# Decode attention with a gated MLP on one core: the small matrix products computed with moving weights in column groups

## The chip, the core and the metric

The kernel runs on one core of one Trainium2 chip. The metric is the time of one execution in device microseconds. Before the change its median over three runs is 1341.24 us (1341.04 to 1341.56). The profile shows one such execution by engine: PE is TensorE (PEld its weight loads), DVE is VectorE, ACT is ScalarE, POOL is GpSimd, SP is SyncE, which here does nothing but issue DMA transfers.

## The reference

Two batch rows, each with a single new token. One branch is attention over a long cache, the other a two-stage MLP; a sigmoid gate mixes them.

```python
# B = 2, Sq = 1, D = 1024, H = 32, Sk = 16384, Dh = 128, F = 3584; all inputs bf16
g = sigmoid((x * gate_w).sum(-1))
q = (x @ wq).reshape(B, 1, H, Dh)
p = softmax(q . k_cache * Dh ** -0.5)          # per head, over 16384 positions
a = (p . v_cache).reshape(B, 1, H * Dh) @ wo
h = gelu(layernorm(x) @ w1)
hs = shift(h) @ w2      # with one position, the four shifted quarters are all padding: zeros
x1 = x + hs
b = x1 + gelu(layernorm(x1) @ w3) @ w4
out = g * a + (1 - g) * b
```

The caches make up nearly all of the bytes: 2 x 32 heads x 16384 x 128 x 2 bytes is 268 MB for K and as much for V. wq and wo have 8.4 MB each, w3 and w4 7.3 MB each, w1 and w2 2.1 MB each.

## The kernel before

**Units.** The work on the caches is cut into 32 units; a unit is a pair of heads of one batch row, and its K and its V are 8.4 MB each: 128 partitions of 64 KB. One large SBUF tile, `mem`, has five cells of 32 KB a partition. K of even units lies in cells 0 and 1, K of odd units in cells 1 and 2, V in cells 3 and 4 (the V of unit 30 in cells 0 and 1). Before the units begin, cells 3 and 4 hold wq, cell 2 holds w1 and w2; then w3 comes into cells 3 and 4 over wq, then w4 over w3, then V of unit 0 over w4. So each of these transfers waits until PE has read what it overwrites.

**The queue.** All loads are issued by SP in one order: wq, x, gate_w, w1, w2, K0, w3 (two halves), K1, the first pair of wo, w4 (two halves), K2, V0 (two halves), K3, V1, K4, V2 and so on. An issue that waits holds up all behind it. K of unit n+1 is issued when the first half of the scores of unit n has been transposed, since the two share a cell.

**A unit (loop at L630).** `score_chunks` (L454) transposes K in eight chunks on DVE (L462, 32x32 blocks of 32-bit words) and multiplies each on PE with 8 weight loads and 8 matmuls of 512 columns (L468), all into one PSUM bank `S`. `softmax_a` transposes S (L489), takes the maximum (L491) and spreads it through a diagonal matrix made by ACT (L493); `softmax_b` sums that on PE (L499), reduces it on DVE (L505) and computes the exponentials on ACT (L507); `softmax_c` sums them on PE (L521) and takes the reciprocal on DVE (L523). `pv_moving` (L539) multiplies the probabilities with V two units later: V moves, 512 columns at a time, through four column groups of the PE array (the output lies at partitions 0, 32, 64 and 96 of the PSUM bank `oacc`), with the 8 probabilities of a position group as weights. `pv_rows` (L554) masks and adds the four parts of `oacc` on DVE, and a small matmul with `hsel` (L590, L585) sums the partitions. After each second unit `wo_project` (L438) adds the heads' part of the output to `arow`, a PSUM tile in which the 1024 output columns lie as four column groups of 256.

**The q product and the MLP layers.** q (L266 to L275) and `LinearT.compute` (L228) use weights as the stationary operand: for each 128 output columns and each 128 rows a weight load of 128x128 and a matmul of only 2 columns (the two batch rows). The outputs then lie along the partitions, as later steps want them. For the MLP layers the 128 columns of one weight load are a column step of C elements apart in memory (C = 8 for w1, w2 and w4, 28 for w3). The q result is spread over partitions by four matmuls with the selection matrices `sel` (L141) into `qd`, of which POOL makes the padded weights `qw` (L301).

**Where the third and fourth layer stand.** w3 is loaded and computed in two halves of its rows. In unit 0 the first half is computed in two parts around `softmax_b` (L640, L642), the second after `softmax_c` (L645); w4's halves are loaded as w3's become free (L643, L646). Unit 1 does the same with w4, and loads the two halves of V0 as w4's become free (L652, L655). The order of the instructions of one engine is worked out by the framework's scheduler, which also moves matmuls of the layers between those of the scores.

**The end.** The V of the last unit comes in nine pieces (`PIECES`, L106: seven of 32 position blocks and two of 16), and then four pieces of wo (L432). `pv_last` (L603) uses the first three pieces as moving operand and the other six as stationary (L612), adds the masked sum of the moving part first (L609), scales (L619) and projects the last two head pairs (L620). DVE copies one half of the columns of `arow` to SBUF, ACT the other (L677, L678), and two stores follow, one per batch row (L680).

Of the kernel before, what the change touches and what calls it, by code (L numbers as in the profile page):

```python
# [10 lines left out]
FP32 = mybir.dt.float32  # L11
# [12 lines left out]
def kernel(  # L24
# [74 lines left out]
    def load_v(u):  # L99
        nc.sync.dma_start(out=region(v_cell[u], NJ * Dh), in_=cache_rows(A_v_cache, u))  # L100

    def load_v_half(u, k):
        at = slice(k * CELL, (k + 1) * CELL)
        nc.sync.dma_start(out=region(v_cell[u], NJ * Dh)[:, at], in_=cache_rows(A_v_cache, u)[:, at])

    PIECES = [32] * 7 + [16] * 2  # L106
    assert sum(PIECES) == NJ

# [29 lines left out]
    ones_f = const.tile([P, P], FP32)  # L138
    nc.vector.memset(ones_f[:], 1.0)

    sel = const.tile([P, 4, Q4, QP], BF16)  # L141
    nc.gpsimd.memset(sel[:], 0.0)
    for v in range(4):
        w, e = divmod(v, 2)
        nc.gpsimd.affine_select(
            out=sel[:, v],
            in_=sel[:, v],
            compare_op=ALU.not_equal,
            fill=1.0,
            base=-(2 * QP * w + e),  # L150
            pattern=[[0, Q4], [-2, QP]],
            channel_multiplier=1,
        )
    mask4 = const.tile([P, Q4], BF16)
    nc.gpsimd.memset(mask4[:], 1.0)
    nc.gpsimd.affine_select(
# [46 lines left out]
    for k in range(NP):  # L203
        t = const.tile([P, NJ // 4, 2, 4], BF16, name=f"pt{k}")
        nc.gpsimd.memset(t[:], 0.0)
        pts.append(t)

    class LinearT:

        def __init__(self, W, actT, name, cell, offset, nparts=1):  # L210
            self.actT = actT
            K, self.N = W.shape
            self.R = K // P
            self.C = self.N // P
            self.rows = self.R // nparts
            self.src = W.rearrange("(p r) n -> p (r n)", p=P)

            self.at = [(cell + k) * CELL + offset for k in range(nparts)]
            self.acc = mlp.tile([P, self.C, B], FP32, name=f"{name}_acc")

        def part(self, k):
            return mem[:, self.at[k] : self.at[k] + self.rows * self.N]

        def load(self, k=0):
            n = self.rows * self.N
            nc.sync.dma_start(out=self.part(k), in_=self.src[:, k * n : (k + 1) * n])

        def compute(self, k, c0, c1):  # L228
            wc = self.part(k).rearrange("p (r n) -> p r n", n=self.N)
            ps = misc_psum([P, c1 - c0, B])  # L230
            for c in range(c0, c1):
                for r in range(self.rows):
                    nc.tensor.matmul(  # L233
                        ps[:, c - c0, :],
                        lhsT=wc[:, r, :].rearrange("p (m c) -> p c m", c=self.C)[:, c, :],
                        rhs=self.actT[:, k * self.rows + r, :],
                        start=(r == 0),
                        stop=(r == self.rows - 1),
                    )
            acc = self.acc[:, c0:c1, :]  # L240
            if k == 0:
                nc.vector.tensor_copy(out=acc, in_=ps[:])
            else:
                nc.vector.tensor_tensor(out=acc, in0=acc, in1=ps[:], op=ALU.add)

    xn1T = mlp.tile([P, KC, B], BF16)
    hT = mlp.tile([P, KC, B], BF16)
# [5 lines left out]

    lin1 = LinearT(B_w1, xn1T, "w1", 2, 0)
    lin2 = LinearT(B_w2, shT, "w2", 2, KC * D)
    lin3 = LinearT(B_w3, xn2T, "w3", 3, 0, 2)
    lin4 = LinearT(B_w4, h2T, "w4", 3, 0, 2)
    lin1.load()
    lin2.load()
    load_k(0)  # L260
# [1 line left out]
    xT = const.tile([P, KC, B], BF16)  # L262
    nc.vector.tensor_copy(out=xT[:], in_=xin[:].rearrange("p b r -> p r b"))  # L263

    qps = misc_psum([P, H, B])
    for h in range(H):  # L266
        for r in range(KC):
            nc.tensor.matmul(  # L268
                qps[:, h, :],
                lhsT=wq_t[:, r, h * Dh : (h + 1) * Dh],  # L270
                rhs=xT[:, r, :],
                start=(r == 0),
                stop=(r == KC - 1),
            )
    lin3.load(0)  # L275
    lin3.load(1)
    qT = const.tile([P, H, B], BF16)
    nc.vector.tensor_copy(out=qT[:], in_=qps[:])
    qdps = misc_psum([P, 4, H * B])
    for v in range(4):  # L280
        nc.tensor.matmul(
            qdps[:, v, :],
            lhsT=sel[:, v].rearrange("p a k -> p (a k)"),
            rhs=qT[:].rearrange("p h b -> p (h b)"),
            start=True,
            stop=True,
        )

    qd = const.tile([P, HP, B, 4], BF16)
    for e in range(2):  # L290
        rows = slice(e * HALF, (e + 1) * HALF)
        nc.vector.tensor_copy(
            out=qd[rows],
            in_=qdps[rows].rearrange("p v (hp e b) -> p hp e b v", e=2, b=B)[:, :, e],
        )
    qdu = qd[:].rearrange("p hp b v -> p (hp b) v")

    def write_qw(u):
# [82 lines left out]
        layernorm_T(x1T[:], xn2T[:], "ln2")  # L381


    NQ = D // Q4
    arow_t = rps.tile([P, NQ], FP32, name="arow")
    nc.vector.memset(arow_t[:], 0.0)
    arow = [arow_t[QP * k : QP * k + B, :] for k in range(Q4)]

    def mlp_post4():

        omg = mlp.tile([P, B], FP32, name="omg")
        nc.vector.tensor_scalar(
            out=omg[:], in0=g_rep[:], scalar1=-1.0, scalar2=1.0, op0=ALU.mult, op1=ALU.add
        )
        nc.vector.tensor_tensor(out=bT[:], in0=lin4.acc[:], in1=x1T[:], op=ALU.add)
        nc.vector.tensor_tensor(
            out=bT[:], in0=bT[:], in1=omg[:].unsqueeze(1).to_broadcast([P, KC, B]), op=ALU.mult
        )
        W = NQ // KC
        for k in range(Q4):  # L400
            for c in range(KC):
                nc.tensor.matmul(  # L402
                    arow[k].rearrange("b (m c) -> b c m", c=KC)[:, c, :],
                    lhsT=bT[:, c, :],
                    rhs=ident_f[:, k * W : (k + 1) * W],
                    start=(c == 0),
                    stop=False,
                    skip_group_check=True,
                )
# [27 lines left out]

    def wo_project(hp):  # L438
        for r in range(2):
            for k in range(Q4):  # L440
                nc.tensor.matmul(
                    arow[k],
                    lhsT=OT[:, hp, r, :],
                    rhs=wo_tiles[hp, r][:, k * NQ : (k + 1) * NQ],
                    start=False,
                    stop=(hp == HP - 1 and r == 1),
                    skip_group_check=True,
                )
# [154 lines left out]
    def pv_last(u):  # L603
        hp, b = units[u]
        ot = misc_psum([P, 2])
        moving = sum(PIECES[:3]) // 4
        pv_moving(u, 0, moving, moving)
        red = pv_rows(u, mask4m)
        nc.tensor.matmul(ot[:], lhsT=red[:, 0:Dh], rhs=hsel[:], start=True, stop=False)  # L609
        V = v_view(u)  # L610
        for j in range(4 * moving, NJ):
            nc.tensor.matmul(  # L612
                ot[:],
                lhsT=V[:, j, :],
                rhs=pts[u % NP][:, j // 4, :, j % 4],
                start=False,
                stop=(j == NJ - 1),
            )
        nc.vector.tensor_tensor(out=OT[:, hp, :, b], in0=ot[:], in1=rinvs[u % NP][:], op=ALU.mult)  # L619
        for k in range(HP - LASTP, HP):  # L620
            wo_project(k)

    compute_gate()
    layernorm_T(xT[:], xn1T[:], "ln1")
    lin1.compute(0, 0, lin1.C)
    mlp_post1()
    lin2.compute(0, 0, lin2.C)
    mlp_post2()

    for n in range(NU):  # L630
# [6 lines left out]
        softmax_a(n)  # L637
        if n == 0:
            load_wo_pair(0)
            lin3.compute(0, 0, FC // 2)  # L640
            softmax_b(n)
            lin3.compute(0, FC // 2, FC)  # L642
            lin4.load(0)  # L643
            softmax_c(n)
            lin3.compute(1, 0, FC)  # L645
            lin4.load(1)  # L646
            gelu_T(lin3.acc[:], h2T[:], FC)
        elif n == 1:
            lin4.compute(0, 0, KC // 2)
            softmax_b(n)  # L650
            lin4.compute(0, KC // 2, KC)
            load_v_half(0, 0)  # L652
            softmax_c(n)
            lin4.compute(1, 0, KC)
            load_v_half(0, 1)  # L655
            mlp_post4()
        else:
            pv(n - 2)
            if n < NU - 1:
                load_v(n - 1)  # L660
            else:
                load_v_pieces(NU - 1)
            pv_end(n - 2)
            if n == NU - 1:
                load_wo_last()
            softmax_b(n)
            softmax_c(n)
# [3 lines left out]
    pv_end(NU - 2)  # L671
    pv_last(NU - 1)

    out_row = mlp.tile([P, NQ], BF16)
    used = slice(0, QP * (Q4 - 1) + B)
    half = NQ // 2
    nc.vector.tensor_copy(out=out_row[used, 0:half], in_=arow_t[used, 0:half])  # L677
    nc.scalar.activation(out=out_row[used, half:NQ], in_=arow_t[used, half:NQ], func=ACTF.Copy)  # L678
    for b, queue in ((0, nc.sync), (1, nc.scalar)):
        queue.dma_start(  # L680
            out=out[b, 0].rearrange("(k n) -> k n", k=Q4),
            in_=out_row[b : b + QP * (Q4 - 1) + 1 : QP, :],
        )


# [28 lines left out]
```

## Time and profile before

| what | value |
|---|---|
| median of three runs | 1341.24 us |
| the profiled execution | 1341.09 us, its span 1339.4 us |
| PE busy / PEld / DVE / ACT | 768.8 / 351.9 / 705.1 / 105.2 us |
| moved by DMA | 573.33 MB, mean 428 GB/s over the span |
| L268 (q), 256 matmuls | 7.1 us busy |
| L233 (layers), weight loads, 576 | 36.9 us busy |
| last V piece used by PE (L612) | 1332.80 us |
| last stores issued (L680) | 1336.49 us |

The page gives busy times of the engines, the share of the DMA engines in 40 equal slices of the span, a chain that follows the last instruction back to what released it, and groups of instructions with their mean duration. The timeline lists instructions in order of time, merged: start, time until the end of the last of them, engine, line, operation, output and inputs, count, and in brackets the idle time of the engine before them with what ended it. "Clock" is the TensorE clock that was granted, as a part of full speed.

### The profile page before, as it was taken

What the parts mean: (1) busy time and instruction counts of PE and PEld (TensorE: products, weight loads), DVE (VectorE), ACT (ScalarE), POOL (GpSimd) and SP (SyncE); (2) the same over time, 40 slices, a digit from 0 to 9 for tenths busy, and PEclk for the clock granted to TensorE, in tenths of its full rate; (3) what the DMA queues carried; (4) which work ended last, traced back from release to release, by engine and by line L of the source; (5) the groups of instructions that cost most, each with busy time, mean ns of one, the idle gap of its engine ahead of it and who ended that gap; (6) DMA issues with size and microseconds to landing.
All of it is one profiled execution on the core that took longest, in us unless ns stands there. A gap on an engine that the chain in (4) does not pass through costs nothing.

```text
span 1339.4 us, 12490 instructions
## 1 busy us (share of the span) xinstructions
PE 768.8 (57%) x5502; PEld 351.9 (26%) x5502; DVE 705.1 (53%) x695; ACT 105.2 (8%) x165; POOL 15.2 (1%) x54
## 2 busy tenths in 40 slices
PE   2688566554566645556654546665455665555564
PEld 2456222222222212222222212222122222222222
DVE  1445566554556554556655445656444665545561
ACT  0011000000000000000000000000000000000000
POOL 1000000000000000000000000000000000000000
PEclk9977887776788777788877778877678886777886
DMA  9999999999999999999999999999999999999997
GB/s 406 425 429 432 440 431 433 435 423 440 429 435 437 429 429 437 425 435 435 435 431 429 429 437 431 429 427 430 440 431 431 427 433 423 437 435 435 433 423 309
DMA packets 14486, 573.33 MB, mean 428 GB/s; under 512 B 1880, under 2 KB 1888, under 8 KB 4448
## 3 DMA queue, kind: packets, MB, share of 16 engines
q1 hardware_dynamic: 14424, 572.54, 99.3%
q8 instruction: 43, 0.70, 0.2%
q14 instruction: 11, 0.09, 0.0%
q10 hardware_dynamic: 8, 0.00, 0.0%
HBM read 572.53 MB, written 0.00 MB: 427 GB/s over the span
## 4 chain that ended last, share of the span: by engine, by line
DMA 67%; PE 16%; DVE 12%; issue 4%; ACT 0%; another core or an unknown queue 0%; POOL 0%; SPq 0%; ACTq 0%; DVEq 0%
DMA mem<-in_A_k_cache_dram 62%; PE S L468 12%; DVE KT L462 12%; PE misc L233 2%; DMA mem<-in_A_v_cache_dram 2%; DMA xin<-in_A_x_dram 2%; DMA wo<-in_A_wo_dram 1%; PE misc L268 1%; ACT pt L507 0%; PE arow L402 0%; PE oacc L543 0%; DVE St L489 0%; POOL ln_rstd L350 0%; PE misc L344 0%
## 5 line engine op out<-in xcount | busy, mean ns | idle before, releaser
L468 PE MATMUL S<-KT,qw 128*128 128x512 bf16 x2048 | 544.2, 415 | 369.5 <-DVE KT L462 369.3
L462 DVE STREAM_TRANSPOSE KT<-mem 128x2048 f32<-128x2048 f32 x256 | 570.9, 2283 | 271.7 <-DMA mem<-in_A_k_cache_dram 219.5
L468 PEld LDWEIGHTS <-qw 128*128 128x128 bf16 x2048 | 217.7, 107 | 688.3 <-issue 509.2
L543 PE MATMUL oacc<-mem,pt 128*8 128x512 bf16 x2008 | 116.9, 384 | 8.7 <-DMA mem<-in_A_v_cache_dram 8.7
L507 ACT ACTIVATE pt<-St,nb 64x256 bf16<-64x256 f32 x64 | 90.0, 1406 | 149.5 <-DVE nb L505 148.6
L493 ACT ACTIVATE Dm<-ident_s,m 128x128 f32<-128x128 f32 x32 | 12.8, 401 | 998.8 <-DVE m L491 998.8
L521 PE MATMUL misc<-rs,lmat 128*128 128x1 f32 x62 | 18.2, 362 | 85.8 <-ACT pt L507 85.6
L543 PEld LDWEIGHTS <-pt 128*8 128x8 bf16 x2008 | 46.4, 87 | 76.2 <-issue 25.9
L489 DVE STREAM_TRANSPOSE St<-S 128x512 f32<-128x512 f32 x32 | 22.9, 717 | 66.6 <-PE S L468 66.6
L523 DVE RECIPROCAL rinv<-misc 128x1 f32<-128x1 f32 x31 | 5.2, 169 | 96.3 <-PE misc L521 96.3
L559 DVE TENSOR_SCALAR part<-oacc,maskr 128x128 f32<-128x128 f32 x31 | 10.9, 351 | 83.0 <-PE oacc L543 83.0
L590 PE MATMUL misc<-hsel,red 128*128 128x2 f32 x112 | 17.5, 261 | 51.5 <-DVE red L565 51.5
L521 PEld LDWEIGHTS misc<-rs,lmat 128*128 128x128 f32 x62 | 15.5, 310 | 94.2 <-ACT pt L507 94.2
L233 PEld LDWEIGHTS <-mem 128*128 128x128 bf16 x576 | 36.9, 169 | 2.2 <-issue 1.4
L590 PEld LDWEIGHTS misc<-hsel,red 128*128 128x128 f32 x112 | 15.9, 202 | 64.8 <-issue 62.6
L507 ACT ACTIVATION_READ_ACCUMULATOR pt<-St,nb 64x1 f32 x64 | 30.7, 480 | 0.0
L565 DVE SCALAR_TENSOR_TENSOR part<-oacc,maskr,part 128x128 f32<-128x128 f32 x62 | 21.8, 351 | 2.2
L268 PE MATMUL misc<-xT,mem 128*128 128x2 bf16 x256 | 7.1, 165 | 26.1 <-DVE xT L263 23.5
L301 POOL TENSOR_TENSOR qw<-qd,mask 128x16 bf16<-128x16 bf16 x32 | 8.4, 264 | 1188.1 <-PE S L468 1159.5
L599 DVE CAST OT<-misc 64x2 bf16<-64x2 f32 x56 | 9.0, 160 | 22.9 <-PE misc L590 22.6
L499 PE MATMUL misc<-Dm,ones_f 128*128 128x128 f32 x64 | 16.5, 343 | 3.5 <-ACT Dm L493 3.5
L505 DVE TENSOR_REDUCE nb<-misc 64x1 f32<-64x64 f32 x64 | 14.2, 222 | 5.5 <-PE misc L499 3.5
(97 smaller groups left out, 150.7 us busy)
## 6 DMA issues: line engine op xcount, KB each, us to landing
mem<-in_B_w_dram SPq DMA_DIRECT2D x4, 3584.0 KB, 18.8
mem<-in_A_v_cache_dram SPq DMA_DIRECT2D x2, 4096.0 KB
wo<-in_A_wo_dram SPq DMA_DIRECT2D x7, 1024.0 KB, 32.4
mem<-in_A_v_cache_dram SPq DMA_DIRECT2D x7, 1024.0 KB, 24.7
mem<-in_B_w_dram SPq DMA_DIRECT2D x2, 2048.0 KB, 28.6
mem<-in_A_v_cache_dram SPq DMA_DIRECT2D x2, 512.0 KB, 17.9
wo<-in_A_wo_dram SPq DMA_DIRECT2D x4, 256.0 KB, 12.8
mem<-in_A_k_cache_dram SPq DMA_DIRECT2D x32, 28.2
```

What stands on the lines that cost most here:

```text
L233: nc.tensor.matmul(ps[:, c - c0, :], lhsT=wc[:, r, :].rearrange("p (m c) -> p c m", c=self.C)[:, c, :], rhs=self.actT[:, k * self.rows + r ...
L268: nc.tensor.matmul(qps[:, h, :], lhsT=wq_t[:, r, h * Dh : (h + 1) * Dh], rhs=xT[:, r, :], start=(r == 0), stop=(r == KC - 1),)
L462: nc.vector.transpose(out=kt[:], in_=Kc.rearrange("p j d -> p (j d)").bitcast(FP32))
L468: nc.tensor.matmul(S, lhsT=t[:, v, NG - 1 - m : NG - 1 - m + P], rhs=ktb[:, half * GT : (half + 1) * GT, w, :, e], start=(first and n == 0 ...
L489: nc.vector.transpose(out=st[:].rearrange("p j r -> p (j r)"), in_=S[:])
L499: nc.tensor.matmul(R_ps[:], lhsT=ones_f[:], rhs=Dm[:], start=True, stop=True)
L505: nc.vector.tensor_reduce(out=nb[rows], in_=R_ps[rows, rows], axis=AX.X, op=ALU.min)
L507: nc.scalar.activation(out=Pt[rows, :, e, :].rearrange("p (m a) k -> p a k m", a=GT // 4), in_=st[rows, :, 0:NG].rearrange("p (a k) m -> p ...
L521: nc.tensor.matmul(tot_ps[:, 0:1], lhsT=lmat[:], rhs=rs[:], start=True, stop=True)
L543: nc.tensor.matmul(acc[QP * q : QP * q + 8, :], lhsT=pts[u % NP][:, g].rearrange("p h k -> p (h k)"), rhs=v_view(u)[:, 4 * g : 4 * g + 4, ...
L565: nc.vector.scalar_tensor_tensor(out=red[:] if twice else part[:], in0=in0.unsqueeze(1).to_broadcast([P, 2, Dh]) if twice else in0, scalar ...
L590: nc.tensor.matmul(ot[:, r, :], lhsT=red[:, r : 2 * Dh : 2], rhs=hsel[:], start=True, stop=True,)
```

## The change

The q product and the four layers swap the roles of their operands. The 2 columns of the activations become the stationary operand, and the weights move, up to 512 columns in a matmul, in four column groups, accumulating in the two banks of `oacc`. The result lies in rows 0 and 1 of each group of 32 partitions; DVE transposes the whole bank in 32x32 blocks (`flipped`) and copies the wanted columns. With that the outputs lie along the partitions as before. `sel` and its matmuls are gone. For q the moving columns are runs of 128 contiguous ones, and column groups 0 and 1 compute the same heads, as do 2 and 3; for the layers the columns of a matmul step by C elements.

w3 and w4 are loaded and computed whole: the third layer after the scores of unit 0, w4's load behind it; the fourth layer in unit 1, and V0's load, whole, behind it. In the program after scheduling the third layer's matmuls stand behind all scores of unit 0 and ahead of its softmax sum; the fourth layer's stand behind the sum of exponentials (L508 in the changed kernel) of unit 1.

In the last unit all pieces of V but the last two move, and the masked sum is added after the stationary part. In the program after scheduling, both pairs of the last projection stand behind that. `arow` becomes two tiles, each of two rows and 512 columns, in column groups 0 and 1 of two PSUM banks; each of DVE and ACT copies and stores one of them.

```diff
-    sel = const.tile([P, 4, Q4, QP], BF16)
-    nc.gpsimd.memset(sel[:], 0.0)
-    for v in range(4):
...
+    def flip():
+        flips[0] += 1
+        return oacc[flips[0] % 2]
+
+    def flipped(acc, view):
+        t = mlp.tile([P, 512], FP32, tag="flip", name="flip")
+        src = view(acc)
+        n = src.shape[1] * src.shape[2] * (src.shape[3] if len(src.shape) > 3 else 1)
+        nc.vector.transpose(out=t[:, 0:n], in_=src)
+        return t[:, 0:n].rearrange("p (c k) -> p c k", k=QP)[:, :, 0:B]
...
-        def compute(self, k, c0, c1):
-            wc = self.part(k).rearrange("p (r n) -> p r n", n=self.N)
-            ps = misc_psum([P, c1 - c0, B])
-            for c in range(c0, c1):
-                for r in range(self.rows):
-                    nc.tensor.matmul(
-                        ps[:, c - c0, :],
-                        lhsT=wc[:, r, :].rearrange("p (m c) -> p c m", c=self.C)[:, c, :],
-                        rhs=self.actT[:, k * self.rows + r, :],
...
+        def compute(self):
+            wc = self.dst.rearrange("p (r g k c) -> p r g c k", g=Q4, k=QP, c=self.C)
+            step = min(self.C, 512 // QP)
+            while self.C % step:
+                step -= 1
+            for c0 in range(0, self.C, step):
+                acc = flip()
+                for r in range(self.R):
+                    for g in range(Q4):
+                        nc.tensor.matmul(
+                            acc[QP * g : QP * g + B, 0 : step * QP],
+                            lhsT=self.actT[:, r, :],
+                            rhs=wc[:, r, g, c0 : c0 + step, :],
+                            start=(r == 0),
+                            stop=(r == self.R - 1),
+                        )
+                got = flipped(
+                    acc, lambda a: a[:, 0 : step * QP].rearrange("p (c k) -> p c k", k=QP)
+                )
+                nc.vector.tensor_copy(out=self.acc[:, c0 : c0 + step, :], in_=got)
...
+    qd = const.tile([P, HP, B, 4], BF16)
+    HG = 512 // Dh
+    for h0 in range(0, HP, HG):
+        acc = flip()
         for r in range(KC):
+            for g in range(Q4):
+                nc.tensor.matmul(
+                    acc[QP * g : QP * g + B, :],
+                    lhsT=xT[:, r, :],
+                    rhs=wq_t[:, r, :].rearrange("p (hp e d) -> p hp e d", e=2, d=Dh)[
+                        :, h0 : h0 + HG, g // 2, :
+                    ],
+                    start=(r == 0),
+                    stop=(r == KC - 1),
+                )
+        got = flipped(acc, lambda a: a[:].rearrange("p (c k e) -> p c e k", k=QP, e=2))
         nc.vector.tensor_copy(
+            out=qd[:, h0 : h0 + HG],
+            in_=got.rearrange("p (hp v) b -> p hp b v", v=4),
+        )
+    lin3.load()
...
-    NQ = D // Q4
-    arow_t = rps.tile([P, NQ], FP32, name="arow")
-    nc.vector.memset(arow_t[:], 0.0)
-    arow = [arow_t[QP * k : QP * k + B, :] for k in range(Q4)]
+    NH2 = D // 512
+    arow_t = [rps.tile([QP * k + B, 512], FP32, name=f"arow{k}") for k in range(NH2)]
+    arow = [arow_t[k][QP * k : QP * k + B, :] for k in range(NH2)]
...
-            for k in range(Q4):
+            for k in range(NH2):
                 nc.tensor.matmul(
                     arow[k],
                     lhsT=OT[:, hp, r, :],
-                    rhs=wo_tiles[hp, r][:, k * NQ : (k + 1) * NQ],
+                    rhs=wo_tiles[hp, r][:, k * 512 : (k + 1) * 512],
...
     def pv_last(u):
-        moving = sum(PIECES[:3]) // 4
+        moving = sum(PIECES[:-2]) // 4
         pv_moving(u, 0, moving, moving)
         red = pv_rows(u, mask4m)
-        nc.tensor.matmul(ot[:], lhsT=red[:, 0:Dh], rhs=hsel[:], start=True, stop=False)
...
+        for k in range(HP - LASTP, HP - 1):
+            wo_project(k)
+        nc.tensor.matmul(ot[:], lhsT=red[:, 0:Dh], rhs=hsel[:], start=False, stop=True)
         nc.vector.tensor_tensor(out=OT[:, hp, :, b], in0=ot[:], in1=rinvs[u % NP][:], op=ALU.mult)
-        for k in range(HP - LASTP, HP):
-            wo_project(k)
+        wo_project(HP - 1)
...
         if n == 0:
             load_wo_pair(0)
-            lin3.compute(0, 0, FC // 2)
+            lin3.compute()
+            lin4.load()
             softmax_b(n)
-            lin3.compute(0, FC // 2, FC)
-            lin4.load(0)
+            gelu_T(lin3.acc[:], h2T[:], FC)
             softmax_c(n)
-            lin3.compute(1, 0, FC)
-            lin4.load(1)
-            gelu_T(lin3.acc[:], h2T[:], FC)
         elif n == 1:
-            lin4.compute(0, 0, KC // 2)
+            lin4.compute()
+            load_v(0)
             softmax_b(n)
-            lin4.compute(0, KC // 2, KC)
-            load_v_half(0, 0)
+            mlp_post4()
             softmax_c(n)
-            lin4.compute(1, 0, KC)
-            load_v_half(0, 1)
-            mlp_post4()
...
-    nc.vector.tensor_copy(out=out_row[used, 0:half], in_=arow_t[used, 0:half])
-    nc.scalar.activation(out=out_row[used, half:NQ], in_=arow_t[used, half:NQ], func=ACTF.Copy)
...
+    nc.vector.tensor_copy(out=out_row[0:B, :], in_=arow[0])
+    nc.sync.dma_start(out=rows[:, 0:512], in_=out_row[0:B, :])
+    nc.scalar.activation(out=out_row[QP : QP + B, :], in_=arow[1], func=ACTF.Copy)
+    nc.scalar.dma_start(out=rows[:, 512:1024], in_=out_row[QP : QP + B, :])
```

More of the change, by code (lines that the diff above doesn't have):

```diff
@@ L100, in load_v @@
         nc.sync.dma_start(out=region(v_cell[u], NJ * Dh), in_=cache_rows(A_v_cache, u))
-    def load_v_half(u, k):
-        at = slice(k * CELL, (k + 1) * CELL)
-        nc.sync.dma_start(out=region(v_cell[u], NJ * Dh)[:, at], in_=cache_rows(A_v_cache, u)[:, at])
     PIECES = [32] * 7 + [16] * 2
@@ L139 @@
     nc.vector.memset(ones_f[:], 1.0)
-    sel = const.tile([P, 4, Q4, QP], BF16)
-    nc.gpsimd.memset(sel[:], 0.0)
-    for v in range(4):
[L144 to L153, printed above, removed]
     mask4 = const.tile([P, Q4], BF16)
@@ L206, with __init__ @@
         pts.append(t)
+    flips = [0]
+    def flip():
[7 more added lines that the diff above has]
+        return t[:, 0:n].rearrange("p (c k) -> p c k", k=QP)[:, :, 0:B]
     class LinearT:
-        def __init__(self, W, actT, name, cell, offset, nparts=1):
+        def __init__(self, W, actT, name, cell, offset):
             self.actT = actT
@@ L214, in __init__ @@
             self.C = self.N // P
-            self.rows = self.R // nparts
             self.src = W.rearrange("(p r) n -> p (r n)", p=P)
-            self.at = [(cell + k) * CELL + offset for k in range(nparts)]
+            at = cell * CELL + offset
+            self.dst = mem[:, at : at + self.R * self.N]
             self.acc = mlp.tile([P, self.C, B], FP32, name=f"{name}_acc")
[L221 to L226, printed above, removed]
@@ L228, in compute, with load @@
-        def compute(self, k, c0, c1):
-            wc = self.part(k).rearrange("p (r n) -> p r n", n=self.N)
-            ps = misc_psum([P, c1 - c0, B])
-            for c in range(c0, c1):
-                for r in range(self.rows):
-                    nc.tensor.matmul(
-                        ps[:, c - c0, :],
-                        lhsT=wc[:, r, :].rearrange("p (m c) -> p c m", c=self.C)[:, c, :],
-                        rhs=self.actT[:, k * self.rows + r, :],
[L237 to L244, printed above, removed]
+        def load(self):
+            nc.sync.dma_start(out=self.dst, in_=self.src)
@@ L255 @@
     lin2 = LinearT(B_w2, shT, "w2", 2, KC * D)
-    lin3 = LinearT(B_w3, xn2T, "w3", 3, 0, 2)
-    lin4 = LinearT(B_w4, h2T, "w4", 3, 0, 2)
+    lin3 = LinearT(B_w3, xn2T, "w3", 3, 0)
+    lin4 = LinearT(B_w4, h2T, "w4", 3, 0)
     lin1.load()
@@ L263 @@
     nc.vector.tensor_copy(out=xT[:], in_=xin[:].rearrange("p b r -> p r b"))
-    qps = misc_psum([P, H, B])
-    for h in range(H):
+    qd = const.tile([P, HP, B, 4], BF16)
+    HG = 512 // Dh
+    for h0 in range(0, HP, HG):
+        acc = flip()
         for r in range(KC):
[L268 to L286, printed above, removed]
-        )
[L289 to L295, printed above, removed]
+            for g in range(Q4):
[9 more added lines that the diff above has]
+        got = flipped(acc, lambda a: a[:].rearrange("p (c k e) -> p c e k", k=QP, e=2))
+        nc.vector.tensor_copy(
+            out=qd[:, h0 : h0 + HG],
+            in_=got.rearrange("p (hp v) b -> p hp b v", v=4),
+        )
+    lin3.load()
     qdu = qd[:].rearrange("p hp b v -> p (hp b) v")
@@ L398, in mlp_post4 @@
         )
-        W = NQ // KC
-        for k in range(Q4):
+        W = 512 // KC
+        for k in range(NH2):
             for c in range(KC):
@@ L439, in wo_project @@
         for r in range(2):
-            for k in range(Q4):
+            for k in range(NH2):
                 nc.tensor.matmul(
@@ L615, in pv_last @@
                 rhs=pts[u % NP][:, j // 4, :, j % 4],
-                start=False,
-                stop=(j == NJ - 1),
-            )
+                start=(j == 4 * moving),
+                stop=False,
+            )
+        for k in range(HP - LASTP, HP - 1):
+            wo_project(k)
+        nc.tensor.matmul(ot[:], lhsT=red[:, 0:Dh], rhs=hsel[:], start=False, stop=True)
         nc.vector.tensor_tensor(out=OT[:, hp, :, b], in0=ot[:], in1=rinvs[u % NP][:], op=ALU.mult)
-        for k in range(HP - LASTP, HP):
-            wo_project(k)
+        wo_project(HP - 1)
     compute_gate()
     layernorm_T(xT[:], xn1T[:], "ln1")
-    lin1.compute(0, 0, lin1.C)
+    lin1.compute()
     mlp_post1()
-    lin2.compute(0, 0, lin2.C)
+    lin2.compute()
     mlp_post2()
@@ L672 @@
     pv_last(NU - 1)
[L674 to L683, printed above, removed]
+    out_row = mlp.tile([QP + B, 512], BF16)
+    rows = out.rearrange("b s d -> (b s) d")
+    nc.vector.tensor_copy(out=out_row[0:B, :], in_=arow[0])
+    nc.sync.dma_start(out=rows[:, 0:512], in_=out_row[0:B, :])
+    nc.scalar.activation(out=out_row[QP : QP + B, :], in_=arow[1], func=ACTF.Copy)
+    nc.scalar.dma_start(out=rows[:, 512:1024], in_=out_row[QP : QP + B, :])
 _INS = ['A_x', 'A_k_cache', 'A_v_cache', 'A_wq', 'A_wo', 'B_x', 'B_w1', 'B_w2', 'B_w3', 'B_w4', 'gate_w']
```

## The prediction

> **What bounds the kernel now.** I read the page's slices, then the chain of waits, then windows over the trace.
>
> ```profile
> DMA  9999999999999999999999999999999999999997
> ...
> DMA 67%; PE 16%; DVE 12%; issue 4%; ACT 0%; another core or an unknown queue 0%; POOL 0%; SPq 0%; ACTq 0%; DVEq 0%
> ```
> ```profile
> 52.00:92.00 40.00, 32.00 (x292) 21.69 (x292) 21.28 (x20) 3.46 (x6) 0.26 (x1) 0.87 1.00 428
> 92.00:132.00 40.00, 33.53 (x355) 23.49 (x355) 23.66 (x23) 3.52 (x6) 0.26 (x1) 0.76 1.01 433
> 172.00:1324.00 1152.00, 657.61 (x4169) 275.71 (x4167) 630.20 (x587) 93.03 (x145) 7.13 (x27) 0.78 1.00 431
> ```
> The last two columns of a window are the busy share of the DMA engines and GB/s. They stand at 1.00 and about 430 in the stage of the MLP as in the steady loop. In the packet records of the trace all 16 engines have a packet in flight from 1.9 us until the tail, and a 64 KB packet takes 2.42 us (16 x 65,536 B / 2.42 us = 433 GB/s). So the time is bytes over that rate, plus the head, plus the tail. PE or DVE time saved in between buys nothing; PE time added costs only when it makes SP issue a transfer after the queue has run dry. So I read SP's issues in the timeline next:
>
> ```profile
> 64.42 0.33 SPq L97 DMA_DIRECT2D mem<-in_A_k_cache_dram  x1
> ...
> 83.35 7.85 SPq L226 DMA_DIRECT2D mem<-in_B_w_dram  x2
> 102.99 0.33 SPq L97 DMA_DIRECT2D mem<-in_A_k_cache_dram  x1
> 121.31 7.77 SPq L104 DMA_DIRECT2D mem<-in_A_v_cache_dram  x2
> ```
> In the packet records these transfers (K1, w4, K2, V0) move their first packets at 68.17, 90.37, 107.12 and 126.09, when the work queued ahead is drained. The very first transfer needed 1.0 us from issue (0.79) to packet (1.81). So the latest harmless issues are 67.1, 89.3, 106.1 and 125.1; w3, issued at 33.1, has until 49.5.
>
> **Head: q, first and second layer.** Removed: 256 q matmuls (23.48 to 33.2), four `sel` matmuls and three casts; 2 x 64 matmuls of the layers at 62 ns (7.97 us). Added: 128 q matmuls of 512 columns, 2 x 32 of 256, and six flips. Four column groups at once are in the trace at V:
>
> ```profile
> 1255.96 3.63 PE L543 MATMUL oacc<-mem,pt 128*8 128x512 bf16 x64
> ...
> 1312.92 6.60 PE L543 MATMUL oacc<-mem,pt 128*8 128x512 bf16 x80 [8.65 <-DMA mem<-in_A_v_cache_dram]
> ...
> 1313.30 0.14 PEld L543 LDWEIGHTS <-pt 128*8 128x8 bf16 x4 [0.28 <-issue]
> ```
> Warm, a round of four takes 3.63/16 = 0.227 us; after an idle PE 0.14+0.28 = 0.42, for some ten rounds. q: 32 rounds, 10 x 0.42 + 22 x 0.227 = 9.2 us, so it ends near 32.7 and w3 goes out where it does now, 16 us early. A flip is like L489's transpose of 128x512 from PSUM, 0.72 us; the four hide under the next rounds but for the last. A layer of 8 rounds of 256 columns takes 8 x 0.21 = 1.7 cold plus about 0.6 for flip and copy, against 4.15; xn2T is ready near 45 instead of 49.9. All of it hides behind K0, whose last packet ends at 52.97: 0. At the price of the old strided weight loads (4 us a layer, the bound above) xn2T is ready near 51: still 0. POOL loses `sel`, DVE the clearing of arow; neither queue is waited for before 23 us: 0.
>
> **Third layer and w4.** In place of 224 matmuls, part of them woven between the scores of unit 0, 64 of 448 columns run after those scores. Without them unit 0 should go like a late unit: first K transpose 1234.24, last score 1256.0, 21.8 us; 53.45 + 21.8 = 75.3. Its 16 rounds at 448/512 x 0.227 = 0.20 take 3.2 us, so w4, now one transfer instead of two, goes out at 78.5 (limit 89.3). The weights step 56 bytes between columns, and no moving operand of the trace does; the nearest in step are L233's weight loads:
>
> ```profile
> 23.48 6.09 PE L268 MATMUL misc<-xT,mem 128*128 128x2 bf16 x223 [23.48 <-DVE xT L263]
> ...
> 38.00 7.77 PEld L233 LDWEIGHTS <-mem 128*128 128x128 bf16 x128 [1.40 <-issue]
> ```
> 61 ns for 128 stepped columns against 27 for contiguous ones. At 0.48 ns a column for all four groups together the layer costs 64 x 448 x 0.48 = 13.8 us, w4 goes out at 89.1: just in time. So 0 at both ends here.
>
> **Fourth layer and V0: the thin place.** V0 overwrites the weights, so it waits for the whole layer. PE's order in the changed program puts the 112 matmuls behind the normalising sum (L521), which waits for ACT's exponentials; the halves of the old layer stood around it:
>
> ```profile
> 121.41 0.50 PEld L521 LDWEIGHTS misc<-rs,lmat 128*128 128x128 f32 x2 [0.22 <-ACT pt L507]
> ...
> 121.65 6.99 PEld L233 LDWEIGHTS <-mem 128*128 128x128 bf16 x112
> ```
> K1's last packet ends at 89.5; transposes from 90.0, scores until 111.8 (21.8 as above). Last score to the sum's end took 115.7 to 122.0, so 6.3: the layer starts at 118.1 on a cold PE. 28 rounds of 256 columns at 0.21 = 6.0 us, so V0 goes out at 124.1, 1.0 us before the limit: 0. Ends of the range: 28 x 0.113 = 3.2 us warm (0 as well); or 112 x 256 x 0.48 = 13.8 us by L233. In that case the third layer's 13.8 us also push the softmax of unit 0, whose reciprocal stands ahead of K1's transposes on DVE: they begin near 94.2, scores end at 116.0, the layer runs from 122.3 to 136.1, and DMA stands still for 11.0 us. I take the cold L543 row, alike in form and state. Behind V0 on SP stands K3, due 14 us later in the old run; K2's transposes on DVE wait for the layer's flip and bT, done near 126, and K2 lands at 128.5.
>
> [...]
>
> **Bytes and packets.** Order rows for PE fall from 10,494 to 9,239. Instruction fetch (0.79 MB for 12,490 instructions, 64 B each) shrinks by 80 KB, five 16 KB packets of 1.07 us: 5 x 1.07/16 = -0.33 us. w3, w4 and V0 move in packets twice as large: 512 packets of 28 KB at 1.064 us become 256 at about 2.12 (-0.13), 256 of 32 KB at 1.215 become 128 at 2.42 (-0.08).
>
> **Tail.**
>
> ```profile
> 1332.80 0.59 PE L612 MATMUL misc<-pt,mem 128*128 128x2 bf16 x16 [0.68 <-DMA mem<-in_A_v_cache_dram]
> ...
> 1333.42 0.16 DVE L619 TENSOR_TENSOR OT<-misc,rinv 128x2 bf16<-128x2 f32 x1 [10.34 <-PE misc L612]
> ...
> 1335.42 0.38 PE L441 MATMUL arow<-wo,OT 128*2 128x256 bf16 x4 [0.26 <-DMA wo<-in_A_wo_dram]
> ...
> 1335.86 0.29 DVE L677 CAST out_row<-arow 98x128 bf16<-98x128 f32 x1 [2.27 <-PE arow L441]
> 1336.18 0.28 ACT L678 ACTIVATE out_row<-arow 98x128 bf16<-98x128 f32 x1 [32.82 <-DVE out_row L677]
> 1336.49 1.35 ACTq L680 DMA_DIRECT2D out_dram<-out_row  x1
> ```
> The last wo piece decides, not V. Four V pieces turn from 32 stationary matmuls (1.01 us) into 8 moving ones (two rounds, 0.6 to 1.0), 2.45 us apart: hidden. The masked sum now follows the seventh piece: 1330.3 + 1.0 + 1.65 (as 1321.45 to 1323.09) = 1333.0; its product with hsel runs behind the last V matmul, 1333.4 to 1333.8, and OT is written at 1334.06 instead of 1333.58. The last two pieces of wo land at 1334.78 and 1335.42: 0.7 us of cover, beyond which lateness would count in full. Two groups of 512 columns take 0.43 cold where four of 256 took 0.21: +0.21 on the last one (0 if warm). Copies: DVE by L278's 64 columns (0.22) and L677's 128 (0.29) is 1.1 ns a column, so 512 take 0.71; ACT from L678 by 0.5 to 0.8 ns a column 0.47 to 0.6. Now ACT waits for DVE and both stores wait for ACT, 0.63 us after the matmuls; then each engine copies and stores its own half, ACT, whose store ends last, after 0.6, DVE after 0.7. Together +0.2 (0 to +0.5).
>
> **Sum.** Span 1339.4 - 0.33 - 0.21 + 0.2 = 1339.06. The profiled run took 1341.09 around its span (+1.69), and the median stands 0.15 higher: 1340.9.
>
> **Rivals.** *Forecast, no change to speak of* (0.74): 1340.3 to 1341.8. *V0 late* (0.18): slower from the point where the fourth layer takes over 7.0 us, 62 ns a matmul where I have 53. If column groups with stepped weights ran two at a time, 56 x 0.21 = 11.8 us, the gap is 4.9 and the time 1345.8; at L233's rate 1352. For it: the thin place, and the 61 ns row; against: four streams together at V. *A tail that gets longer* (0.05): OT behind the last wo piece by up to 0.5, copies one after the other as now, +0.6: about 1342; L677 to L678 speaks for it, two separate PSUM tiles against. *A real gain* (0.03): the woven layers were in somebody's way after all; the full DMA share from 12 to 1324 us leaves only head and tail, some 6 us, so 1338 at best.
>
> This kernel can't tell less than about 0.2%, 2.7 us, from no change. Of V0-late I put 0.04 below that: same 0.74 + 0.04 + 0.05 = 0.83, slower 0.14, faster 0.03. Range 1340.2 to 1346.0: it takes in two-at-a-time and leaves out L233's price (about 0.06) and the gain.
>
> **What would show it.** V0's issue before 125 and DMA at 1.00 in 92 to 172 us: right; a slice below and V0 after 126: the rival. Also w4's issue near 79, the old landing of K0 and K1, the last wo matmul to the stores in about 0.8 us more or less unchanged. A DMA gap anywhere else, or packets slower than 2.42 us, would make the whole reasoning wrong.

## The result and the profile after

The changed kernel takes 1346.62 us (median of six runs, 1346.15 to 1347.11) against 1341.16 (six runs of the kernel before): 5.5 us more, a ratio of 1.004 with a 95% interval of 1.0027 to 1.0053. The profiled execution took 1346.30 us, its span 1344.5 against 1339.4.

Windows of the trace after, over the stage of the MLP and over the steady loop (the last three columns are granted clock, DMA share and GB/s):

```profile
52.00:92.00 40.00, 30.53 (x132) 8.95 (x132) 22.09 (x23) 3.46 (x6) 0.27 (x1) 0.88 0.99 423
92.00:132.00 40.00, 30.81 (x180) 10.96 (x179) 19.83 (x15) 3.21 (x5) 0.26 (x1) 0.83 0.86 370
...
172.00:1324.00 1152.00, 663.24 (x4052) 274.26 (x4055) 630.22 (x579) 93.07 (x145) 7.17 (x27) 0.77 1.00 432
```

One window alone lost DMA time: 0.86 where the kernel before had 1.01. Narrower windows show an outright stop, with PE busy all through it:

```profile
126.00:128.00 2.00, 2.00 (x24) 0.67 (x20) 0.00 (x0) 0.00 (x0) 0.00 (x0) 1.00 0.04 8
128.00:130.00 2.00, 2.00 (x21) 0.54 (x16) 0.00 (x0) 0.00 (x0) 0.00 (x0) 1.00 0.00 0
130.00:132.00 2.00, 2.00 (x20) 0.41 (x12) 0.00 (x0) 0.00 (x0) 0.00 (x0) 1.00 0.00 0
```

The timeline after, for the third layer with w4's issue and for the fourth with V0's:

```profile
74.89 12.39 PE L231 MATMUL oacc<-mem,xn2T 128*2 128x448 bf16 x64
...
87.32 0.33 SPq L219 DMA_DIRECT2D mem<-in_B_w_dram  x1
...
119.22 12.88 PE L231 MATMUL oacc<-mem,h2T 128*2 128x256 bf16 x112
...
132.14 0.33 SPq L100 DMA_DIRECT2D mem<-in_A_v_cache_dram  x1
```

The fourth layer takes 12.9 us, not 6. V0, which overwrites its weights, goes out at its end, 132.1, when more than half of the DMA engines have had no packet for 5.5 us (the last one ran dry at 128.1); its first packets follow a microsecond later. By the packet records fewer than half of the DMA engines are at work from 126.66 to 133.24, 6.6 us. Everything later is DMA-bound again, so none of it comes back. The rest of the difference goes the other way. The last load ends at 1340.22 instead of 1334.95; without the 6.6 us that would be 1333.6, 1.3 earlier. And from that point to the end of the span it is 4.28 us instead of 4.45. 6.6 - 1.3 - 0.2 = 5.1, the difference of the spans.

### The profile page after: what moved, and what is told of

Same layout as the page of the kernel before. It is cut to its first block, busy times and chain, and to the rows that moved or that the text cites. A ratio compares the mean times of both kernels' runs of the same rounds, so it can differ in the third digit from the quotient of the medians.

```text
span 1344.5 us, 11160 instructions
## 1 busy us (share of the span) xinstructions
PE 776.2 (58%) x4842; PEld 315.2 (23%) x4842; DVE 710.1 (53%) x701; ACT 105.2 (8%) x165; POOL 13.8 (1%) x49
## 4 chain that ended last, share of the span: by engine, by line
DMA 67%; PE 15%; DVE 13%; issue 4%; another core or an unknown queue 0%; ACT 0%; POOL 0%; SPq 0%; DVEq 0%; ACTq 0%
DMA mem<-in_A_k_cache_dram 62%; DVE KT L449 12%; PE S L455 11%; DMA mem<-in_A_v_cache_dram 3%; PE oacc L231 2%; DMA xin<-in_A_x_dram 2%; PE oacc L269 1%; ACT pt L494 0%; DVE flip L203 0%; PE arow L428 0%; POOL ln_rstd L338 0%; PE misc L508 0%; PE misc L332 0%; DVE St L476 0%
## 5 line engine op out<-in xcount | busy, mean ns | idle before, releaser
L530 PE MATMUL oacc<-mem,pt 128*8 128x512 bf16 x2040 | 122.0, 392 | 16.1 <-DMA mem<-in_A_v_cache_dram 16.1
L480 ACT ACTIVATE Dm<-ident_s,m 128x128 f32<-128x128 f32 x32 | 12.9, 402 | 1000.7 <-DVE m L478 1000.7
L508 PE MATMUL misc<-rs,lmat 128*128 128x1 f32 x62 | 18.0, 359 | 86.8 <-ACT pt L494 86.8
L508 PEld LDWEIGHTS misc<-rs,lmat 128*128 128x128 f32 x62 | 15.4, 308 | 101.2 <-ACT pt L494 101.2
L203 DVE STREAM_TRANSPOSE flip<-oacc 128x512 f32<-128x512 f32 (+2 forms) x9 | 5.5, 613 | 34.0 <-PE oacc L231 28.4
L269 PE MATMUL oacc<-mem,xT 128*2 128x512 bf16 x128 | 8.8, 445 | 23.2 <-DVE xT L260 23.2
```

Source lines behind the costliest of these rows:

```text
L269: nc.tensor.matmul(acc[QP * g : QP * g + B, :], lhsT=xT[:, r, :], rhs=wq_t[:, r, :].rearrange("p (hp e d) -> p hp e d", e=2, d=Dh)[:, h0 : ...
L508: nc.tensor.matmul(tot_ps[:, 0:1], lhsT=lmat[:], rhs=rs[:], start=True, stop=True)
L530: nc.tensor.matmul(acc[QP * q : QP * q + 8, :], lhsT=pts[u % NP][:, g].rearrange("p h k -> p (h k)"), rhs=v_view(u)[:, 4 * g : 4 * g + 4, ...
```

## The experiments

The kernel before was timed along with each group of runs: 1341.05, 1341.18 and 1341.19 us.

**Contiguous runs (e1_contig).** The same columns of weights, in the order in which they lie in memory, so that only the place of the step changes:

```diff
-            wc = self.dst.rearrange("p (r g k c) -> p r g c k", g=Q4, k=QP, c=self.C)
+            wc = self.dst.rearrange("p (r g k c) -> p r g k c", g=Q4, k=QP, c=self.C)
-                            rhs=wc[:, r, g, c0 : c0 + step, :],
+                            rhs=wc[:, r, g, :, c0 : c0 + step],
-                    acc, lambda a: a[:, 0 : step * QP].rearrange("p (c k) -> p c k", k=QP)
+                    acc, lambda a: a[:, 0 : step * QP].rearrange("p (k c) -> p c k", k=QP)
```

> All four layers keep their moving weights in four column groups, but the columns of one matmul are taken in the order in which they lie in memory (runs of 8 or 14 contiguous columns, k outer and c inner), and DVE's transpose reads the PSUM bank with a step instead. Theory (the step between columns makes a round slow, the round makes the fourth layer long, the layer makes V0 late): rounds of 256 columns fall from 0.45 us to 0.11 to 0.21, the fourth layer from 12.9 us to 6 or less, V0 goes out before 125.1, no DMA gap, 1340.5 us (1340.0 to 1341.2). Rival 1 (four groups with 2-column weights are slow in the layers whatever the step, for instance by their many weight loads): rounds stay at 0.45 and the time at 1346.6. Rival 2 (the step only moves from the matmul to DVE, whose transposes become long): the layer is short, V0 early, and the time is 1340.5 too, unless a transpose takes over 5 us.

Measured: 1339.32 us (1339.02 to 1339.51), ratio to before 0.9987 (0.9977 to 0.9997). It is faster than both kernels, and 1.2 us faster than expected. The timeline of this run, third and fourth layer, V0's issue and the transpose that now reads PSUM with a step:

```profile
74.31 3.27 PE L231 MATMUL oacc<-mem,xn2T 128*2 128x448 bf16 x64
...
117.06 4.93 PE L231 MATMUL oacc<-mem,h2T 128*2 128x256 bf16 x112
...
122.04 0.33 SPq L100 DMA_DIRECT2D mem<-in_A_v_cache_dram  x1
122.05 0.45 DVE L203 STREAM_TRANSPOSE flip<-oacc 128x256 f32<-128x256 f32 x1 [4.39 <-PE oacc L231]
```

12.39 us became 3.27, 12.88 became 4.93, V0 goes out 3 us before the limit, and the transpose takes the same 0.45 us with the step as without. So the step of the moving operand is what made the layers long; the four groups and their 2-column weights did not.

**V0 in halves (e2_v0_halves).** The layer stays slow, V0's first half no longer waits for all of it:

```diff
             lin4.compute()
-            load_v(0)
+            load_v_half(0, 0)
+            load_v_half(0, 1)
```

> The changed kernel with one edit: V0 is loaded in its two halves again. The first half overwrites only the first 16 of the 28 rows of w4 that a partition holds, so it may go out after 16 of 28 rounds: 119.2 + 16 x 0.452 = 126.5 instead of 132.1, the second after all. The layer itself is untouched. Theory (the whole loss is the time in which V0 is not yet issued and DMA stands still): the gap shrinks from 7.0 us to about 1.4, so 1346.6 - 5.6 = 1341.0 us (1340.7 to 1342.0). Rival (the slow layer costs elsewhere too, through K2's transposes or K3's issue): 1344 to 1346.6.

Measured: 1341.00 us (1340.48 to 1341.56), ratio 1.0 (0.999 to 1.0009). The first half goes out at 126.84 and the gap is 1.4 us (126.51 to 127.89). Without that gap it would be 1339.6, 0.3 above e1. So a fourth layer of 12.9 us costs next to nothing by itself; the wait of V0 for its end is the loss.

**Old operands in the new places (e3_old_whole_late).** The kernel before, with

```diff
-    lin4 = LinearT(B_w4, h2T, "w4", 3, 0, 2)
+    lin4 = LinearT(B_w4, h2T, "w4", 3, 0)
...
-            lin4.compute(0, 0, KC // 2)
             softmax_b(n)
-            lin4.compute(0, KC // 2, KC)
-            load_v_half(0, 0)
             softmax_c(n)
-            lin4.compute(1, 0, KC)
-            load_v_half(0, 1)
+            lin4.compute(0, 0, KC)
+            load_v(0)
             mlp_post4()
```

and the third layer whole in the same manner.

> The kernel before, with its old operands (weights stationary, 224 matmuls of 62 ns for each of the last two layers), but with w3, w4 and V0 loaded whole, the third layer whole after the scores of unit 0 and the fourth whole after the sum of exponentials of unit 1, as in the changed kernel. Theory (the new layers are as slow as the old ones, and the loss comes from waiting for a whole late layer): the fourth layer takes 224 x 0.062 = 13.9 us from about 121, V0 goes out near 135.5, a gap of about 10 us, 1351 us (1348.5 to 1352). Rival (the loss comes with the operand swap; old operands in the new places would do no harm): 1341.2 us.

Measured: 1349.31 us (1348.68 to 1350.29), ratio 1.0063 (1.0048 to 1.0078). Its timeline:

```profile
121.09 13.59 PE L233 MATMUL misc<-h2T,mem 128*128 128x2 bf16 x224
...
134.71 0.17 DVE L242 COPY w_acc<-misc 128x16 f32<-128x16 f32 x1 [12.96 <-PE misc L233]
```

The old layer takes 13.6 us where the changed one takes 12.9, and DMA stands still for 8.0 us (127.81 to 135.84). So the changed layers were no slower than the old; the old kernel hid the same length by weaving, and by letting w4 and V0 follow in halves. Which of the two did how much for the old operands was not tried.

**Rates of the moving operand (e4_probe).** The changed kernel with bursts ahead of q, such as

```diff
+    for r in range(8):
+        for g in (0, 1, 2, 3):
+            nc.tensor.matmul(pacc[QP * g : QP * g + B, 0:256], lhsT=pw[:],
+                rhs=mem[:, g * 2048 : g * 2048 + 255 * 8 + 1 : 8], start=True, stop=True, ...
```

> The changed kernel with bursts of matmuls ahead of q, on a zeroed stretch of the empty K cell, while wq is still on its way: 256 moving columns and 2-column weights; 18 rounds of four groups with contiguous columns to warm up, then 8 rounds each of four groups with a step of 1, 2, 4 and 8 elements, one group with step 8, two groups with step 8, four groups with step 28, one group with step 1. The results are overwritten by q. [...] Theory B (streams with a step go one after the other through a shared path): step 8 with four groups 0.45, two groups 0.23, one group 0.11. In both, the time stays at that of the changed kernel within 1 us, since q has 16 us of cover.

Measured: 1346.79 us in its one run, as the changed kernel. The timeline, weight loads and matmuls of the bursts with four groups and steps of 2 (L268), 4 (L272) and 8 elements (L276), and of the one group with step 8 (L280):

```profile
12.96 1.18 PE L268 MATMUL oacc<-mem,pw 128*2 128x256 bf16 x32
13.88 2.12 PE L272 MATMUL oacc<-mem,pw 128*2 128x256 bf16 x32
15.72 3.89 PE L276 MATMUL oacc<-mem,pw 128*2 128x256 bf16 x32
19.33 2.88 PE L280 MATMUL oacc<-mem,pw 128*2 128x256 bf16 x6
```
```profile
17.08 0.20 PEld L276 LDWEIGHTS <-pw 128*2 128x2 bf16 x4 [0.25 <-issue]
17.53 0.20 PEld L276 LDWEIGHTS <-pw 128*2 128x2 bf16 x4 [0.25 <-issue]
...
20.24 0.10 PEld L280 LDWEIGHTS <-pw 128*2 128x2 bf16 x1 [0.35 <-issue]
20.69 0.10 PEld L280 LDWEIGHTS <-pw 128*2 128x2 bf16 x1 [0.35 <-issue]
```

From start to start of the bursts, eight rounds each: step 2 takes 0.92/8 = 0.115 us a round, step 4 1.84/8 = 0.23, step 8 3.61/8 = 0.45. The second fence shows the period: 0.45 us for four matmuls side by side (L276), and 0.45 for a single one (L280). Two groups with step 8 also take 0.45. So each stream is slowed by its own step, and four slow streams still run together; by theory B the single group would have taken 0.11. The contiguous burst behind the warm-up (L264) still holds slow rounds (1.31/8 = 0.16 us on average), so it gives no rate; e1's third layer does, 3.27/16 us for 448 contiguous columns, which is 0.117 for 256. Step 28 came out at 0.44 to 0.49.

**One layer at a time (e5_only_w4_runs, e6_only_w3_runs).** Runs in the fourth layer alone, and in the third alone: the edit of e1, made to depend on the layer's name.

> The changed kernel with contiguous runs in the fourth layer alone; the other three keep the step. Theory (one layer decides, by the moment at which V0 can go out): the third layer still takes 12.4 us, unit 1 is late as in the changed kernel, the fourth starts near 119.2 and takes 4.9 us as in the run with runs everywhere; V0 goes out at 124.2, before the limit of 125 to 126, no gap, 1339.3 us (1339.0 to 1340.3). Rival (each slow layer costs its share): more than 1341.

> The changed kernel with contiguous runs in the third layer alone. Theory: the fourth starts near 117.1 as in the run with runs everywhere and takes 12.9 us; V0 goes out at 130.0, a gap of 4.4 to 4.9 us, 1339.3 + 4.6 = 1343.9 us (1343.2 to 1344.6). Rival (V0's lateness is made by the late start as much as by the layer): nearer to 1340.

Measured: 1339.59 us (1339.07 to 1340.44; ratio 0.999, 0.998 to 0.9999) and 1344.32 us (1344.11 to 1344.68; ratio 1.0024, 1.0014 to 1.0034). V0's issue, in e5 and in e6:

```profile
123.97 0.33 SPq L100 DMA_DIRECT2D mem<-in_A_v_cache_dram  x1
```
```profile
129.97 0.33 SPq L100 DMA_DIRECT2D mem<-in_A_v_cache_dram  x1
```

In e5 the third layer is as slow as in the changed kernel, and there is no gap. In e6 the fourth runs from 117.06, and DMA stands still for 4.6 us. A slow layer ahead of the deadline costs little (0.3 us to e1, about the spread of the runs); V0 6 us later costs 4.6, since e5 had 1.4 to spare.

**The tail alone (e7_tail_only).** The kernel before with the changed `pv_last`, `arow`, copies and stores.

> The kernel before with the end of the changed one (pv_last, the output sum in two column groups, copies and stores); head and layers untouched. From last load to the end of the span, before has 4.45 us and the changed kernel 4.28 in the packet records. Theory (the tail gives 0.2 to 0.3 us, by stores that take less time to issue, 0.53 instead of 1.35 us on ACT): 1340.8 us (1340.5 to 1341.0). Rival (the tail gives all of the 1.7 us by which the kernel with runs beats the one before): 1339.4.

Measured: 1340.77 us (1340.51 to 1341.83), ratio 0.9998 (0.9989 to 1.0007); the median is 0.4 lower than before's, which alone does not tell it from no change. In its profile the last load ends as in the kernel before (1335.01 and 1334.95), so what it gains lies behind that. So the tail is not the 1.7 us.

**The number of instructions (e8_runs_padded, e9_runs_spread, e10_runs_again).** e1 with 660 matmuls of a zero tile added, all ahead of q, or 22 in each of 30 units:

```diff
+            pad = misc_psum([P, B])
+            for r in range(22):
+                nc.tensor.matmul(pad[0:B, :], lhsT=pw[:], rhs=pw[:], start=True, stop=True)
```

> The kernel with runs in all layers, with 660 tiny matmuls of a zero tile ahead of q (1,320 more PE instructions, as many as the change had removed), at a time when PE waits for wq; their result is overwritten. Theory 1 (fetched instructions cost DMA time spread evenly over 16 engines): 1,320 x 64 B are 84 KB, five packets of 1.07 us, 0.34 us, so 1339.65. Theory 2 (the packets of instruction fetch fall on few engines, and the engine that ends last decides; the missing instructions are most of the 1.7 us by which this kernel beats the one before): 1340.3 to 1341.0. Rival (the gain has nothing to do with the number of instructions): 1339.3.

> The kernel with runs in all layers and the same 660 tiny matmuls (1,320 PE instructions), but 22 of them in each of units 2 to 31, behind the softmax, where PE waits some 9 us for K; their result is not read. If the instructions cost what they cost ahead of q, because their fetch takes DMA time at any place: 1340.7 us (1340.4 to 1341.0). If the price ahead of q came from the place (fetch and wq together, or q ending 10 us later): 1339.3 to 1339.7.

> The kernel with runs in all layers once more, unchanged, on the same chip as the run beside it, so that the padded ones have a neighbour: 1339.3 us (1339.0 to 1339.6), V0 issued near 122, no gap.

Measured: 1340.73 us (1340.47 to 1341.10) ahead of q, 1340.61 (1340.39 to 1340.96) spread out, 1339.29 (1339.05 to 1339.48) without, on the same chip as the spread ones. 1,320 instructions that PE has time for cost 1.3 to 1.4 us at both places. The pages' rows for instruction fetch, of e1 and then of e8:

```profile
q8 instruction: 38, 0.62, 0.2%
```
```profile
q8 instruction: 43, 0.70, 0.2%
```

Five packets more, as many as the kernel before has, for 1.4 us: about 0.28 each on average, where the even share that I had worked out was 0.067. But it is no price for each packet: e7 has 385 instructions and two fetch packets less than the kernel before (41), and its last load ends no earlier.

The packet records show why. An engine's next packet starts 3 to 4 ns before its last one ends, so the chain of each engine can be followed. A fetch packet takes its engine 1.07 us, and the 64 KB packet behind it takes 2.92 instead of 2.42: 1.55 us, on one engine alone. At the end not all engines have work left, as windows of the kernel before show (0.57 is nine of 16):

```profile
1328.00:1330.00 2.00, 0.87 (x32) 0.78 (x30) 0.00 (x0) 0.00 (x0) 0.00 (x0) 0.50 0.66 267
1330.00:1332.00 2.00, 1.48 (x48) 1.40 (x48) 0.00 (x0) 0.00 (x0) 0.00 (x0) 0.50 0.57 225
```

In e1 seven engines end their share of the last load by 1328.9, three at 1331.3 to 1331.6, one at 1332.2 and five at 1332.9 to 1333.3. In e8 seven end by 1329.5, one at 1332.1, five at 1333.1 to 1333.3 and three at 1334.2 to 1334.7. That is what packets going round eight engines would give: of 38, the last of which falls behind its engine's data, five engines have five and three have four; of 43, three have six and five have five. In e7, 41 packets leave a single engine with six: one ends at 1335.0, all others by 1333.5. On that reading the load ends with the engine that had most, and five packets more raise that from five to six.

## Why the prediction was wrong

**What bounds the kernel** held. DMA is full but for the gap and the ends; the slow first three layers cost next to nothing, and the 6.6 us lost are those in which SP had not issued. The limit for V0 held within 0.4 us: gaps of 1.4 us for an issue at 126.8, 4.6 for 130.0 and 6.6 for 132.1 put it at 125.3 to 125.5, where I had 125.1. The 126.09 behind that is the start of K2's last packet; V0's first one, of 32 KB, starts at 126.39.

**Head.** q took 8.8 us (9.2 in the sum) and w3 went out at 31.8. The first two layers took 3.8 us each instead of 1.7, the bound by L233's rate, and were hidden, as that bound said.

**Third layer.** It took 12.4 us, near the 13.8 of the bound and not the 3.2 of the sum, and w4 went out at 87.3, ahead of its limit by 1.7 us (w4's first packet of 28 KB starts at 90.03 in the kernel before, not at 90.37, so the limit is 89.0): "just in time", as written.

**Fourth layer: the step that failed.** "28 rounds of 256 columns at 0.21 = 6.0 us, so V0 goes out at 124.1." The start was about right (119.2 against 118.1); a round took 0.45 us, not 0.21. I had two rows, V's four groups (alike in groups, contiguous) and the stepped weight loads (alike in step), and took the one that resembled the change in form. The probe shows that the step sets the rate: 0.45 us for one group as for four. The discarded row, 0.48 ns a column over all groups, comes to 13.8 us against 12.9 measured. With that rate the rival *V0 late* follows by its own working: its deciding point was 7.0 us for the layer, its price at most 11, and 6.6 was paid. The rival's mechanism was right, and I had given it 0.18; its two-at-a-time variant was not what happened. The range ended at 1346.0 because L233's price was left out of it, although it was the one row with a step.

**The step, in numbers.** In the probe a round of 256 columns takes 0.115 us at a step of 2 elements, 0.23 at 4 and 0.45 at 8; e1's third layer gives 0.117 for contiguous columns. So the fourth layer's step of 8 costs nearly four times the contiguous round. I had 0.21 for it, by which the layer still fitted, and at the warm end of the range 0.113, which no run shows for step 8.

**Bytes and packets, mis-sized.** The sum had -0.33 for fewer instructions and -0.21 for larger packets; the last load ended 1.3 us earlier, gap aside. The padded runs put 1.3 to 1.4 us on the instructions alone. What was wrong is the division by 16: a fetch packet delays one engine by 1.55 us, and the ends of the chains fit a load that ends with the engine that had most of them. The -0.21 is not visible: e3 has the larger packets and all the old instructions, and its last load, less its gap, ends at 1335.16, no earlier than before's 1334.95.

**Tail, wrong in sign by a little.** The last matmuls do take 0.19 us longer and the copies 0.65 to 0.71 where it was 0.63, as worked out, here with the timeline after:

```profile
1341.38 0.68 DVE L658 CAST out_row<-arow 2x512 bf16<-2x512 f32 x1 [2.01 <-PE arow L428]
1341.42 0.59 ACT L660 ACTIVATE out_row<-arow 2x512 bf16<-2x512 f32 x1 [32.06 <-PE arow L428]
1342.03 0.53 ACTq L661 DMA_DIRECT2D out_dram<-out_row  x1
1342.09 0.33 SPq L659 DMA_DIRECT2D out_dram<-out_row  x1
```

What the sum did not hold is the stores: two rows of 1 KB take ACT 0.53 us to issue where four rows of 512 bytes took 1.35, and from issue to the end of the span it is 2.47 instead of 2.91. So the tail gains 0.2 where I had +0.2.

**The forecast without its error.** e1 is the kernel that I had in mind, with V0 in time. I had 1340.9 for it with a lower end of 1340.2; it takes 1339.3. Both mis-sized terms, the fetch packets and the tail, erred to the same side; in the changed kernel the earlier last load and the shorter tail took back 1.5 us of the gap's 6.6.

## What to carry to other kernels

In a DMA-bound kernel the price of a slow piece of compute is set by the next transfer that must wait for it: list each transfer's issue against the time at which the queue runs dry, and cost the change there with the slowest row at hand. When the operands of a matmul are swapped, look at what lies next to what in memory: a step that was harmless for stationary weights, because their load (61 ns for 128 stepped columns) was hidden, came back as the rate of the moving operand (0.45 us a round at step 8, 0.117 contiguous). Order the loops so that the moving operand runs through memory, and leave the step to the copy out of PSUM, where it cost nothing here (0.45 us for the transpose with the step as without).

## What the runs showed of the hardware

- The rate of a moving bf16 operand falls to a half when only every fourth element is taken and to a quarter when every eighth is (0.115, 0.23 and 0.45 us for 256 columns at steps of 2, 4 and 8, about 0.117 for contiguous ones); at step 8 one column group takes as long as four. 0.45/256 is 1.76 ns a column at step 8; a step of 28 costs about as much (0.44 to 0.49 us). The granted clock makes no difference at that rate: in the fourth layer a round takes 0.45 us from 119.65 to 131, though the clock was 0.50 until 122 and 1.00 from 123.
- 1,320 additional PE instructions cost 1.3 to 1.4 us in a kernel whose DMA is full, four times what their five fetch packets take if they are shared by 16 engines (5 x 1.07/16 = 0.33). A fetch packet sets back one engine by 1.55 us, and the ends of the chains fit packets that go round eight of the engines; the one with the most ends last. On that reading the price comes in steps: five packets less took one such step away, two less (e7) none. Why eight, the runs do not show.
- In e8, PE stood still for 2.6 to 4.1 us after the first 224 and then after each 128 of the small matmuls, waiting for nothing that the profile names, while the DMA queues were full with wq and what followed:

```profile
12.50 3.34 PE L254 MATMUL oacc<-pw 128*2 128x2 bf16 x128 [4.07 <-issue]
...
25.17 3.34 PE L254 MATMUL oacc<-pw 128*2 128x2 bf16 x128 [2.58 <-issue]
```

  A fetch packet lands 1.3 to 1.6 us before each of the four restarts (at 11.09, 17.83, 23.59 and 30.65), and 128 matmuls with their weight loads, at 64 B each (0.79 MB for 12,490 instructions in the kernel before), are one such packet of 16 KB. That fits a wait for fetched instructions; no run tested it apart.
